# Token pairs, an earlier first group and re-placed weight requests in an FFN beside a long convolution

## The chip, the cores and the metric

The kernel runs on one core of one Trainium2 chip. The metric is device time in microseconds (us) of one execution. TensorE is written PE, its weight loads PEld, VectorE DVE, ScalarE ACT, GpSimd POOL, and SyncE SP; SP here only asks for DMA transfers.

## The reference

For 2048 tokens x of 576 channels the kernel computes a layer norm, a long convolution along the tokens (an S4 kernel applied through a Fourier transform) and a dense layer with SiLU, and adds all three paths.

```
xn  = layernorm(x)
K   = real(sum_n C * dB * exp(dt*A * l))          # 576 x 2048
A   = irfft(rfft(pad(xn)) * rfft(pad(K))) + xn * Dskip
B   = silu(xn @ w1) @ w2                          # w1 576 x 4608, w2 4608 x 576
out = x + A(xn) + B(xn)
```

Everything is float32. Matrix products are made of three products of rounded parts: each operand is split into a high part (a cast on ACT) and a low part (a subtraction on DVE).

## The kernel before

**The dense layer** (`ffn`, line 228, and `wino_ffn`, line 377) is the main program. Tokens are worked in two halves of 1024, each of two blocks `b` of 512; the 4608 hidden channels in 18 chunks `c` of four tiles of 128. A *plain* block (half, c, b) has four up products (`up`, line 278; u0 to u3; 14 matmuls of 512 columns each) and four down products (`down`, line 298; d0 to d3, one for 128 tokens; 24 matmuls of 288 columns each), which DVE adds to the running sum `acc` (line 316). A loop (line 347) writes the downs of one block and the ups of the next in the order u0, d0 to d3, u1, u2, u3. Behind each up stands a *gate*: SiLU into `gf` (line 294), a cast into `gh` (line 295), a subtraction into `gl` (line 296). `gh` and `gl` live in the pool `gp`, with six buffers of each, and a block's four are read until its d3 ends.

**The weights** are asked for by `load_w1` (line 235; one raw buffer `w1r` that holds two tiles) and `load_w2` (line 260; two raw buffers `w2r`), and split by casts (lines 255, 273) and subtractions. There are five buffers each for `w1h`, `w1l`, `w2h`, `w2l`.

**The Strassen phase.** From chunk 2 of the second half on, `wino_ffn` does both blocks together, in 14 groups n = 4 to 17 of two hidden tiles each, with seven block products in place of eight. `wino_x` (line 546) first forms the token sums S1 to S4 on DVE and ACT; its temporaries (pool `sx`) take the memory of the convolution-kernel generator, so it starts behind that generator's last store to `d1k`. For each group the raw `w1r` is cast as it is (parts "c2", "c1"), then summed in place by four DVE instructions (`sums`, lines 403 to 406), then cast again ("t13", "t24"). For the first group these steps stand ahead of the loop (lines 459 to 463), behind the gates of the last plain block, since each cast is issued behind the gate last written (line 389). Within the loop, group n holds the downs of what came before, the two splits of its own w2 tiles (both behind d0), the requests for the next two w2 tiles (both behind d1), the steps of the next group's w1, and at its end (line 536) the request for the w1 after that.

**The convolution** is the side program (`side`, line 973), woven into the main one at fixed places (line 1029). First come layer norm and transposition (`phase0`, with the raw tokens of the second half in `xj`, one buffer), then the convolution kernel (`kgen`), then 32 frequency steps (`spectral`, line 850: loads `ur` and `kr`, products pk and pu, DVE products, a product pb, a store to `d2`; `ka`, `kb`, `yh`, `yl` have one buffer each, and its pool `kl` takes the memory of `sx`), then `tail` (line 897). Only when all 32 have been stored can `conv_load` (line 944) fetch `ys`, 128 tokens at a time, six in flight; `add_conv` (line 951) multiplies them by the last Fourier matrix on parts of the PE array and adds them. Tokens 0 to 7 (times 128; `j` below) are added by `tail` to a sum read back as `r0`, tokens 8 to 15 by `down` itself, ahead of each of its last-step products (line 302).

**What sets the order.** A planner simulates the engines when the program is built and fixes one order for each engine's queue. An instruction is taken as it becomes ready there, in the order of the text; what stands under `high_priority` goes first, and what stands under `behind(ins)` follows `ins` on its engine. An instruction whose tile has no free buffer is held back by the planner. On the chip each queue then runs strictly in its order, so one that waits holds up all behind it.

Of the kernel before, what the change touches and what calls it, by code (L numbers as in the profile page):

```python
# [10 lines left out]
F32 = mybir.dt.float32  # L11
F32R = mybir.dt.float32r
# [5 lines left out]
P = 128  # L18
L = 2048
D = 576  # L20
# [21 lines left out]
def kernel(  # L42
# [185 lines left out]
    def ffn():  # L228
# [69 lines left out]
        def down(blk, jj, terms=None):  # L298
            half, c, b = blk
            j = 8 * half + 4 * b + jj  # L300
            js = slice(jj * P, (jj + 1) * P)
            if half == 1 and c == NCH - 1:
                add_conv(j, acc[j])
                conv_load(j + AHEAD)
            terms = terms or [(G[blk, t], W2[half, c, t]) for t in range(FT)]
            for h in range(2):
                hs = slice(h * HD, (h + 1) * HD)
                po = ps2.tile([P, 512], F32, tag="ps2", name="po")
                n = 0
                for gs, ws in terms:  # L310
                    for g, w in ((0, 0), (0, 1), (1, 0)):
                        pins["pe"] = nc.tensor.matmul(po[:, :HD], gs[g][:, js], ws[w][:, hs],  # L312
                                                      start=n == 0, stop=n == 3 * len(terms) - 1).ins
                        n += 1
                with tc.high_priority():
                    nc.vector.tensor_add(acc[j][:, hs], po[:, :HD], acc[j][:, hs])  # L316
# [25 lines left out]
        for t in range(FT):  # L342
            up(blocks[0], t, 256, 512)
            yield 3.0

        plain = blocks[:2 * (NCH + WINO_C)]
# [28 lines left out]
        yield from wino_ffn(load_w1, load_w2, split_w2, R1, W2, plain[-1], down)  # L375

    def wino_ffn(load_w1, load_w2, split_w2, R1, W2, before, down):
# [5 lines left out]
        G, WT = {}, {}  # L383

        def split(src, name, n):
            h = wp.tile([P, 5, P], F32R, tag="w1h", name="w1h", bufs=FT + 1)
            l = wp.tile([P, 5, P], F32R, tag="w1l", name="w1l", bufs=FT + 1)
            k = src.shape[1]
            with behind(pins["gh"]):
                nc.scalar.copy(h[:, :k], src)  # L390
            nc.vector.tensor_sub(l[:, :k], src, h[:, :k])
            WT[name, n] = h, l

        def raw(n):
            return R1[1, n // 2, n % 2 * 2]

        def sums(n):

            if n >= end:
                return  # L400
            r1 = raw(n)
            b11, b21, b12, b22 = (r1[:, k:k + 2, f:f + P] for f in (0, P) for k in (0, 2))
            nc.vector.tensor_sub(b22, b22, b12)
            nc.vector.tensor_sub(b12, b12, b11)
            nc.vector.tensor_add(b11, b22, b11)
            nc.vector.tensor_sub(b21, b21, b11)

        def prep(n, part):
            if n >= NFT // 2:
                return  # L410
            r1 = raw(n)
            if part == "c1":
                split(r1[:, 0:5, 0:P], "c1", n)
            elif part == "c2":
                split(r1[:, 2:5, P:2 * P], "c2", n)
            elif part == "t13":
                split(r1[:, 0:4, P:2 * P], "t13", n)
            elif part == "t24":
                split(r1[:, 0:4, 0:P], "t24", n)

        def unit(name, n, a):
            h, l = WT[name, n]
# [25 lines left out]
        first, end = WINO_C * FT // 2, NFT // 2  # L448

        def load(n):  # L450
            if n < end:
                load_w1(1, n // 2, n % 2 * 2)

        def second(n, i, part):
            if n < end:
# [28 lines left out]
        for n in range(first, end):  # L484
# [22 lines left out]
            yield 0  # L507
            prod(pb, unit("t13", n, 2), S3)
# [1 line left out]
                nc.vector.tensor_add(f5, pb, f5)  # L510
            d[2]()
            prep(n + 1, "c1")
            sums(n + 1)
            yield 0
            d[3]()
            yield 0

            def lower():
# [378 lines left out]
    def tail():  # L897
# [5 lines left out]
            nc.sync.dma_start(r0s[j], dr0[j * P:(j + 2) * P, :].rearrange("(i p) d -> p i d", p=P))  # L903

        def last(j):
            add_conv(j, r0s[j - j % 2][:, j % 2, :])
            conv_load(j + AHEAD)
            if j % 2:
                store(r0s[j - 1], j - 1, (nc.gpsimd,))
# [34 lines left out]
    def conv_load(j):  # L944
        if j < NJ:
            yss[j] = yp.tile([P, 4, HD], F32, tag="ys", name="ys", bufs=AHEAD)
            for h in range(2):
                nc.sync.dma_start(yss[j][64 * h:64 * h + 64],
                                  d2[j * 256:(j + 1) * 256, h * HD:(h + 1) * HD].rearrange("(q r) d -> r q d", q=4))

    def add_conv(j, dst):

        ys = yss.pop(j)
        py = [pss.tile([P, 512], F32, tag="pss", name="py") for _ in range(2)]
        first = pins["pe"]
        for n in range(8):
            q1, q2, h = n // 4, n // 2 % 2, 1 - n % 2
            o = 64 * q1 + 32 * q2
            rows = slice(64 * h, 64 * h + 64)
            with tc.high_priority() if n else nullcontext(), behind(first):  # L960
                mm = nc.tensor.matmul(py[h][o:o + 32, :HD], s4[rows], ys[rows, 2 * q2 + q1],
                                      start=True, stop=True, tile_position=(64 * h, o), skip_group_check=True)
            if n == 0:
                first = mm.ins
        for h in range(2):
            hs = slice(h * HD, (h + 1) * HD)
            nc.vector.tensor_add(dst[:, hs], py[h][:, :HD], dst[:, hs])

    def gate_of(i):

# [141 lines left out]
```

## Time and profile before

| | |
|---|---|
| device time, three runs | 1154.96 us median (1151.34 to 1156.66) |
| the profiled execution | 1158.77 us, 3.8 us above that median; span of its instructions 1157.0 us |
| plain blocks end, Strassen phase begins on PE | at about 670 us |
| last frequency step stored | at about 1084 us |
| last matmul | ends at about 1152 us |

Times in the views count from the first instruction. A row of the timeline gives start, duration, engine, source line, operation, output<-input, and in brackets the engine's idle time before it with what ended it. A row of the stage view gives, for a stretch, the busy time of each engine with its instructions, then the granted PE clock (1.00 is full), the DMA share and GB/s. A row of the waits gives total us, times, and the longest.

### The profile page before, as it was taken

What the parts mean: (1) busy time and instruction counts of PE and PEld (TensorE: products, weight loads), DVE (VectorE), ACT (ScalarE), POOL (GpSimd) and SP (SyncE); (2) the same over time, 40 slices, a digit from 0 to 9 for tenths busy, and PEclk for the clock granted to TensorE, in tenths of its full rate; (3) what the DMA queues carried; (4) which work ended last, traced back from release to release, by engine and by line L of the source; (5) the groups of instructions that cost most, each with busy time, mean ns of one, the idle gap of its engine ahead of it and who ended that gap; (6) DMA issues with size and microseconds to landing.
All of it is one profiled execution on the core that took longest, in us unless ns stands there. A gap on an engine that the chain in (4) does not pass through costs nothing.

```text
span 1157.0 us, 23107 instructions
## 1 busy us (share of the span) xinstructions
PE 1112.0 (96%) x9101; PEld 992.5 (86%) x9101; DVE 980.7 (85%) x1675; ACT 735.5 (64%) x1297; POOL 100.4 (9%) x178
## 2 busy tenths in 40 slices
PE   6999999999999999999999989999999999999988
PEld 5988898999988888888889878998898899898765
DVE  6699779999999999989999488978888789788425
ACT  4665356667776676766667347877878678677310
POOL 1110000000000000000000010111111111110102
PEclk9999999999999999999999999999999999999979
DMA  9345421424242415264743325444444445443598
GB/s 271 109 138 177 158 76 59 120 72 101 94 107 90 109 60 134 80 191 146 217 132 86 79 59 170 128 133 144 137 128 127 138 131 156 122 145 97 145 233 226
DMA packets 167372, 151.26 MB, mean 131 GB/s; under 512 B 87984, under 2 KB 136128, under 8 KB 166624
## 3 DMA queue, kind: packets, MB, share of 16 engines
q1 hardware_dynamic: 150128, 112.66, 35.0%
q0 software_dynamic: 16752, 36.24, 10.0%
q8 instruction: 72, 1.18, 0.4%
q10 hardware_dynamic: 384, 0.89, 0.3%
q14 instruction: 36, 0.29, 0.1%
HBM read 103.74 MB, written 46.08 MB: 129 GB/s over the span
## 4 chain that ended last, share of the span: by engine, by line
PE 51%; DVE 23%; DMA 10%; ACT 9%; issue 5%; SPq 1%; ACTq 0%; DVEq 0%; POOL 0%; POOLq 0%
PE po L312 22%; PE ph L286 13%; DMA w1r<-in_B_w_dram 4%; PE pb L430 3%; DVE acc L316 2%; DVE C L784 2%; DMA w2r<-in_B_w_dram 2%; DVE th L759 2%; PE kp L816 2%; PE pc L430 1%; DVE gl L296 1%; DVE S L795 1%; DVE th L776 1%; DVE C L795 1%; DMA ys<-d 1%
## 5 line engine op out<-in xcount | busy, mean ns | idle before, releaser
L312 PE MATMUL po<-w2h,gh 128*128 128x288 f32 x1152 | 342.2, 299 | 7.5 <-DVE acc L316 5.6
L312 PE MATMUL po<-w2l,gh 128*128 128x288 f32 x1152 | 339.6, 297 | 0.9 <-DVE w2l L275 0.9
L312 PE MATMUL po<-w2h,gl 128*128 128x288 f32 x1152 | 336.8, 297 | 0.6 <-DVE gl L296 0.6
L312 PEld LDWEIGHTS po<-w2h,gh 128*128 128x128 f32 x1152 | 216.9, 189 | 23.0 <-DVE acc L316 10.1
L312 PEld LDWEIGHTS po<-w2l,gh 128*128 128x128 f32 x1152 | 217.4, 189 | 7.1 <-DVE w2l L275 1.3
L312 PEld LDWEIGHTS po<-w2h,gl 128*128 128x128 f32 x1152 | 216.3, 189 | 3.7 <-issue 1.2
L316 DVE TENSOR_TENSOR acc<-po,acc 128x288 f32<-128x288 f32 x296 | 130.1, 450 | 30.9 <-PE po L312 29.5
L286 PE MATMUL ph<-xh,w1h 128*128 128x512 f32 (+1 forms) x368 | 99.3, 387 | 0.6 <-ACT xh L123 0.6
L286 PE MATMUL ph<-xl,w1h 128*128 128x512 f32 (+1 forms) x368 | 99.8, 386 | 0.0
L286 PE MATMUL ph<-xh,w1l 128*128 128x512 f32 (+1 forms) x368 | 99.8, 382 | 0.0
L294 ACT ACTIVATE gf<-ph 128x512 f32<-128x512 f32 (+1 forms) x92 | 53.2, 578 | 58.8 <-PE ph L288 53.4
L273 ACT CAST w2h<-w2r 128x576 fp32r<-128x576 f32 x72 | 47.3, 673 | 49.4 <-DMA ys<-d 26.5
L286 PEld LDWEIGHTS ph<-xl,w1h 128*128 128x128 f32 x368 | 67.3, 191 | 12.3
L286 PEld LDWEIGHTS ph<-xh,w1l 128*128 128x128 f32 x368 | 66.5, 189 | 11.7
L286 PEld LDWEIGHTS ph<-xh,w1h 128*128 128x128 f32 x368 | 65.8, 191 | 11.2 <-ACT xh L123 0.9
L777 ACT ACTIVATE c<-th 128x1040 f32<-128x1040 f32 x36 | 38.7, 1074 | 49.3 <-DVE th L776 49.2
L296 DVE TENSOR_TENSOR gl<-gf,gh 128x512 fp32r<-128x512 f32 (+1 forms) x92 | 60.5, 660 | 10.8 <-ACT gh L295 10.5
L775 ACT ACTIVATE c<-th,magic 128x1040 f32<-128x1040 f32 x36 | 42.1, 1168 | 41.5 <-DVE C L796 32.6
L853 POOL DMA_DIRECT2D m<-in_cm_dram x64 | 34.6, 542 | 308.0 <-PE pu L941 223.5
L275 DVE TENSOR_TENSOR w2l<-w2r,w2h 128x576 fp32r<-128x576 f32 x72 | 53.4, 749 | 6.2 <-ACT w2h L273 6.1
L295 ACT CAST gh<-gf 128x512 fp32r<-128x512 f32 (+1 forms) x92 | 55.1, 601 | 4.3 <-PE po L312 2.7
L157 POOL DMA_DIRECT2D d1u<-u x32 | 17.4, 543 | 453.5 <-ACT u L156 453.5
(268 smaller groups left out, 2460.3 us busy)
## 6 DMA issues: line engine op xcount, KB each, us to landing
w2r<-in_B_w_dram SPq DMA_DIRECT2D x72, 288.0 KB, 3.6
w1r<-in_B_w_dram SPq DMA_DIRECT2D x35, 512.0 KB, 3.7
d1u<-u POOLq DMA_DIRECT2D x32, 288.0 KB, 2.7
d1k<-stage SPq DMA_DIRECT2D x18, 512.0 KB, 6.9
ur<-d1u SPq DMA_DIRECT2D x32, 288.0 KB, 3.0
kr<-d1k SPq DMA_DIRECT2D x32, 288.0 KB, 2.8
d<-yo POOLq DMA_DIRECT2D x32, 288.0 KB, 2.8
ys<-d SPq DMA_DIRECT2D x32, 288.0 KB, 9.0
```

Source lines behind the costliest of these rows:

```text
L273: pins["w2h"] = nc.scalar.copy(h2, r2).ins
L275: nc.vector.tensor_sub(l2, r2, h2)
L286: nc.tensor.matmul(ph, w[:, kt, :], v[:, kt, a:e], start=n + kt == 0, stop=False)
L294: nc.scalar.activation(gf, ph, AF.Silu)
L295: pins["gh"] = nc.scalar.copy(gh, gf).ins
L296: pins["gl"] = nc.vector.tensor_sub(gl, gf, gh).ins
L312: pins["pe"] = nc.tensor.matmul(po[:, :HD], gs[g][:, js], ws[w][:, hs], start=n == 0, stop=n == 3 * len(terms) - 1).ins
L316: nc.vector.tensor_add(acc[j][:, hs], po[:, :HD], acc[j][:, hs])
L430: pins["pe"] = nc.tensor.matmul(dst, a[:, kt], v[:, kt], start=start and n == 0, stop=stop and n == 5, skip_group_check=True).ins
L775: nc.scalar.activation(c65, th, AF.Identity, bias=magic)
L777: nc.scalar.activation(c65, th, AF.Abs)
L853: nc.gpsimd.dma_start(m, cm23[:, k, i:i + 2])
```

## The change

1. `gp` has five buffers instead of six. In the Strassen phase every sixth gate takes its pair from the pool `xp` instead, which lives from there on. `xj` has two buffers instead of one.
2. The first Strassen group's request for w1 stands behind u0 of the last plain loop pass instead of u2, and its five steps stand behind d1, d2, d3, u1 and u2 of that pass instead of ahead of the Strassen loop. The request for the second group's w1 follows them, at the same place in the text.
3. In a group of the Strassen loop the second w2 split moves from d0 to d3, and each request for a w2 tile of the next group stands right behind the split of this group that frees a raw buffer.
4. In the last step, tokens 8 to 15 get their convolution two at a time, behind the product of the even one: 16 matmuls in one run, the second set in the PSUM pool `ps1`, and the two `ys` requests behind them. Tokens 0 to 7 stay as they were.

```diff
-    gp = ctx.enter_context(tc.tile_pool(name="gp", bufs=6))
+    gp = ctx.enter_context(tc.tile_pool(name="gp", bufs=5))
...
-        t = pool.tile([P, 2, D], F32, tag=tag, name=f"{tag}{j}", **({"bufs": 1} if tag == "xj" else {}))
+        t = pool.tile([P, 2, D], F32, tag=tag, name=f"{tag}{j}")
...
-            if half == 1 and c == NCH - 1:
-                add_conv(j, acc[j])
-                conv_load(j + AHEAD)
...
+            if half == 1 and c == NCH - 1 and jj % 2 == 0:
+                add_conv((j, acc[j]), (j + 1, acc[j + 1]))
+                for i in range(2):
+                    conv_load(j + i + AHEAD)
...
+        early = {"d1": "c2", "d2": "c1", "d3": "sums", "u1": "t13", "u2": "t24"}
...
-                if new == (1, WINO_C) and (b, step) == (0, "u2"):
-                    load_w1(1, WINO_C, 0)
+                if new == (1, WINO_C):
+                    if step == "u0":
+                        load_w1(1, WINO_C, 0)
+                    elif step in early:
+                        prep(first, early[step])
...
-            gh, gl = (gp.tile([P, 512], F32R, tag=n, name=n) for n in ("gh", "gl"))
+            spare = len(G) % 6 == 5
+            gh, gl = ((wino["pool"] if spare else gp).tile([P, 512], F32R, tag=n, name=n) for n in ("gh", "gl"))
...
-        for part in ("c2", "c1"):
-            prep(first, part)
-        sums(first)
-        for part in ("t13", "t24"):
-            prep(first, part)
         load(first + 1)
...
             d[0]()
             second(n, 0, "split")
-            second(n, 1, "split")
+            second(n + 1, 0, "load")
...
             d[1]()
-            second(n + 1, 0, "load")
-            second(n + 1, 1, "load")
             prep(n + 1, "c2")
...
             d[3]()
+            second(n, 1, "split")
+            second(n + 1, 1, "load")
...
-    def add_conv(j, dst):
+    def add_conv(*parts):
...
-        py = [pss.tile([P, 512], F32, tag="pss", name="py") for _ in range(2)]
+        ys = [yss.pop(j) for j, _ in parts]
+        py = [[pool.tile([P, 512], F32, tag=tag, name="py") for _ in range(2)]
+              for pool, tag in ((pss, "pss"), (ps1, "ps1"))[:len(parts)]]
...
-        for n in range(8):
-            q1, q2, h = n // 4, n // 2 % 2, 1 - n % 2
+        for n in range(8 * len(parts)):
+            i, q1, q2, h = n // 8, n // 4 % 2, n // 2 % 2, 1 - n % 2
```

More of the change, by code (lines that the diff above doesn't have):

```diff
@@ L344, in ffn, with split, raw, sums @@
             yield 3.0
+        WT = {}
+        first, end = WINO_C * FT // 2, NFT // 2
+        def split(src, name, n):
+            h = wp.tile([P, 5, P], F32R, tag="w1h", name="w1h", bufs=FT + 1)
+            l = wp.tile([P, 5, P], F32R, tag="w1l", name="w1l", bufs=FT + 1)
+            k = src.shape[1]
+            with behind(pins["gh"]):
+                nc.scalar.copy(h[:, :k], src)
+            nc.vector.tensor_sub(l[:, :k], src, h[:, :k])
+            WT[name, n] = h, l
+        def raw(n):
+            return R1[1, n // 2, n % 2 * 2]
+        def sums(n):
+            r1 = raw(n)
+            b11, b21, b12, b22 = (r1[:, k:k + 2, f:f + P] for f in (0, P) for k in (0, 2))
+            nc.vector.tensor_sub(b22, b22, b12)
+            nc.vector.tensor_sub(b12, b12, b11)
+            nc.vector.tensor_add(b11, b22, b11)
+            nc.vector.tensor_sub(b21, b21, b11)
+        def prep(n, part):
+            if n >= end:
+                return
+            if part == "sums":
+                return sums(n)
+            r1 = raw(n)
+            if part == "c1":
+                split(r1[:, 0:5, 0:P], "c1", n)
+            elif part == "c2":
+                split(r1[:, 2:5, P:2 * P], "c2", n)
+            elif part == "t13":
+                split(r1[:, 0:4, P:2 * P], "t13", n)
+            elif part == "t24":
+                split(r1[:, 0:4, 0:P], "t24", n)
+        early = {"d1": "c2", "d2": "c1", "d3": "sums", "u1": "t13", "u2": "t24"}
         plain = blocks[:2 * (NCH + WINO_C)]
@@ L372, in ffn, with wino_ffn @@
                     f(*new, t)
-                if new == (1, WINO_C) and (b, step) == (0, "u2"):
-                    load_w1(1, WINO_C, 0)
-        yield from wino_ffn(load_w1, load_w2, split_w2, R1, W2, plain[-1], down)
-    def wino_ffn(load_w1, load_w2, split_w2, R1, W2, before, down):
+                if new == (1, WINO_C):
[3 more added lines that the diff above has]
+                        prep(first, early[step])
+        yield from wino_ffn(load_w1, load_w2, split_w2, prep, WT, first, end, W2, plain[-1], down)
+    def wino_ffn(load_w1, load_w2, split_w2, prep, WT, first, end, W2, before, down):
         ps_a = ps1.tile([P, 512], F32, tag="ps1", name="pa")
@@ L382, in wino_ffn @@
         nc.tensor.matmul(ps_a, x40[:, :P], x40, start=True, stop=True)
[L383 to L419, printed above, removed]
+        G = {}
         def unit(name, n, a):
@@ L446, in gate @@
                 pins["gl"] = nc.vector.tensor_sub(gl, gf, gh).ins
-        first, end = WINO_C * FT // 2, NFT // 2
         def load(n):
@@ L454, in second @@
         def second(n, i, part):
-            if n < end:
+            if first <= n < end:
                 f = 2 * n + i
                 (load_w2 if part == "load" else split_w2)(1, f // FT, f % FT)
-        for part in ("c2", "c1"):
-            prep(first, part)
-        sums(first)
-        for part in ("t13", "t24"):
-            prep(first, part)
         load(first + 1)
@@ L512, in wino_ffn @@
             prep(n + 1, "c1")
-            sums(n + 1)
+            prep(n + 1, "sums")
             yield 0
             d[3]()
+            second(n, 1, "split")
+            second(n + 1, 1, "load")
             yield 0
@@ L905, in last @@
         def last(j):
-            add_conv(j, r0s[j - j % 2][:, j % 2, :])
+            add_conv((j, r0s[j - j % 2][:, j % 2, :]))
             conv_load(j + AHEAD)
@@ L960, in add_conv @@
             with tc.high_priority() if n else nullcontext(), behind(first):
-                mm = nc.tensor.matmul(py[h][o:o + 32, :HD], s4[rows], ys[rows, 2 * q2 + q1],
+                mm = nc.tensor.matmul(py[i][h][o:o + 32, :HD], s4[rows], ys[i][rows, 2 * q2 + q1],
                                       start=True, stop=True, tile_position=(64 * h, o), skip_group_check=True)
@@ L964, in add_conv @@
                 first = mm.ins
-        for h in range(2):
-            hs = slice(h * HD, (h + 1) * HD)
-            nc.vector.tensor_add(dst[:, hs], py[h][:, :HD], dst[:, hs])
+        for i, (_, dst) in enumerate(parts):
+            for h in range(2):
+                hs = slice(h * HD, (h + 1) * HD)
+                nc.vector.tensor_add(dst[:, hs], py[i][h][:, :HD], dst[:, hs])
     def gate_of(i):
```

1 line of the change is left out of this document (removed).

## The prediction

> **What bounds the kernel now.** I read the page first.
>
> ```profile
> span 1157.0 us, 23107 instructions
> ...
> PE 1112.0 (96%) x9101; PEld 992.5 (86%) x9101; DVE 980.7 (85%) x1675; ACT 735.5 (64%) x1297; POOL 100.4 (9%) x178
> ```
>
> PE is idle for 45 us in all, and the change removes no matmul; it can win only PE's idle time, time at a low PE clock, and overhead of small matmuls. So I cut the span into stages by what the program does in them.
>
> ```profile
> 0.00:60.00 60.00, 48.60 (x321) 44.79 (x322) 41.32 (x103) 34.24 (x65) 10.86 (x15) 1.00 0.64 183
> 60.00:200.00 140.00, 137.60 (x953) 124.66 (x952) 120.57 (x208) 76.70 (x115) 4.61 (x6) 0.99 0.40 126
> 200.00:655.00 455.00, 447.03 (x4759) 400.87 (x4758) 434.46 (x638) 310.63 (x468) 21.20 (x39) 1.00 0.41 113
> 655.00:712.00 57.00, 50.31 (x295) 43.54 (x295) 42.88 (x68) 28.36 (x50) 3.61 (x6) 0.97 0.37 92
> 712.00:1080.00 368.00, 362.81 (x2249) 330.72 (x2249) 310.96 (x595) 278.61 (x591) 48.87 (x90) 1.00 0.45 133
> 1080.00:1157.00 77.00, 65.64 (x532) 47.89 (x530) 30.50 (x66) 6.98 (x14) 11.24 (x23) 0.88 0.84 220
> ```
>
> PE's idle time is span minus its first number. The two long stages lose 8.0 us in 455 and 5.2 in 368: PE-bound. The passage from plain blocks to Strassen groups loses 6.7 in 57, the end 11.4 in 77, and these two also have a clock under 1.00. There the change works, so I asked who PE waited for: first in the passage, then at the end.
>
> ```profile
> PE pb L430 <- ACT w1h L390: 2.2, 1, 2.2
> PE po L312 <- DVE acc L316: 1.5, 2, 0.9
> PE pa L430 <- ACT pa L490: 1.5, 1, 1.5
> PE pb L436 <- DVE f L510: 1.2, 1, 1.2
> PE pu L941 <- ACT kb L871: 0.3, 1, 0.3
> ```
>
> ```profile
> PE py L961 <- DMA ys<-d: 6.6, 4, 2.6
> ```
>
> The low clock is placed by stretches.
>
> ```profile
> 698.97:702.38 3.41, 1.84 (x9) 1.09 (x8) 3.28 (x8) 3.27 (x8) 0.54 (x1) 1.00 0.03 7
> 702.38:705.80 3.42, 3.42 (x11) 2.77 (x10) 2.85 (x6) 2.77 (x5) 0.00 (x0) 0.50 0.63 196
> ...
> 1098.33:1101.74 3.41, 3.41 (x22) 2.62 (x18) 0.82 (x2) 0.00 (x0) 0.84 (x2) 0.50 1.09 219
> 1108.57:1122.22 13.65, 11.04 (x45) 7.56 (x44) 3.32 (x7) 4.03 (x8) 1.93 (x4) 0.50 0.96 240
> ```
>
> Each half-clock stretch follows one in which PE was often idle: the first follows 3.41 us with 1.84 busy. At half speed it costs 3.42 / 2 = 1.7 us; the two at the end cost up to (3.41 + 13.65) / 2 = 8.5, beside the 6.6 of waits.
>
> **Part 2, the early casts.** ACT's rows show the passage.
>
> ```profile
> 654.74 0.62 ACT L295 CAST gh<-gf 128x512 fp32r<-128x512 f32 x1
> ...
> 670.88 1.13 ACT L390 CAST w1h<-w1r 128x384 fp32r<-128x384 f32 x2
> ...
> 697.97 0.51 ACT L390 CAST w1h<-w1r 128x384 fp32r<-128x384 f32 x1 [3.14 <-DMA w1r<-in_B_w_dram]
> ```
>
> The first group's casts run at 670.88, behind the last plain gate, and PE waits 2.2 for them. In the new place they run behind gates of the block before, in an ACT that is busy 28.36 of 57 us in this stage, and less before d3. That wait goes: **2.2 us**. DVE's groups from 666.8 to 691.1 show the rest.
>
> ```profile
> L552 DVE TENSOR_TENSOR x<-xh,xl 128x1024 f32<-128x1024 f32 x4 | 4.6, 1219 | 1.7 <-DMA d1k<-stage 1.7
> L391 DVE TENSOR_TENSOR w1l<-w1r,w1h 128x512 fp32r<-128x512 f32 (+2 forms) x4 | 2.7, 685 | 0.9 <-ACT w1h L390 0.9
> ...
> L406 DVE TENSOR_TENSOR w1r<-w1r 128x256 f32<-128x256 f32 x1 | 0.4, 415 | 0.0
> L405 DVE TENSOR_TENSOR w1r<-w1r 128x256 f32<-128x256 f32 x1 | 0.4, 414 | 0.0
> L403 DVE TENSOR_TENSOR w1r<-w1r 128x256 f32<-128x256 f32 x1 | 0.4, 409 | 0.0
> L404 DVE TENSOR_TENSOR w1r<-w1r 128x256 f32<-128x256 f32 x1 | 0.4, 409 | 0.0
> ```
>
> DVE is the engine in demand here: the token sums start when the store to `d1k` has landed and then run without a pause. Four w1 subtractions (2.7) and four sums (1.6) stand among them: 4.3 us of DVE leave this stretch. They go to one where DVE waits for PE:
>
> ```profile
> 664.72 0.46 DVE L316 TENSOR_TENSOR acc<-po,acc 128x288 f32<-128x288 f32 x1 [1.15 <-PE po L312]
> ```
>
> so there they cost nothing; if that cover were gone, they cost the same 4.3. Of the 3.0 us that PE waits for `acc` and `pa`, I take half, **1.5** (bounds 0 and 3.0), since DVE keeps its long sums.
>
> The raw `w1r` is freed by the last subtraction of the first group, and SP asks for the second group's weights behind it:
>
> ```profile
> 688.80 0.33 SPq L933 DMA_DIRECT2D ur<-d1u  x1
> ...
> 691.03 0.38 SPq L242 DMA_DIRECT2D w1r<-in_B_w_dram  x1
> ```
>
> It is in time nowhere: ACT stands 3.14 us at the cast of 697.97 with the spectral copies queued behind it, DVE stands behind ACT, the addition of line 510 is late, PE waits 1.2 + 0.3 and loses 1.7 to the clock. With the group free at about 668 the request comes some 20 us sooner. This chain goes: **3.2 us** (bounds 1.5, if the clock dips anyway, and 3.2). PE's total in the passage is 2.2 + 1.5 + 3.2 = 6.9.
>
> The Trainium skill ("TensorE: Matmul & The Clock Gate", Part 1: The HAM clock gate) says that PE falls to half clock after an idle window of about 3.4 us. Here the dip came with 1.84 of 3.41 us busy, so the trace does not agree; by the rule the dip has another cause and stays, and the sum below would be 1.7 us less.
>
> Does PE's gain reach the end? The end hangs on the spectral steps: the last is stored, `ys` is fetched, PE waits.
>
> ```profile
> 1081.65 2.39 DMA d<-yo
> ...
> 1099.57 13.23 DMA ys<-d
> ```
>
> The 32 steps from 688.80 to 1081.65 take 12.3 us each and begin when the token sums give up their memory. If they begin no sooner, PE only waits longer at `ys`. They begin 4.3 us sooner by the DVE work taken out, and up to 3.1 more by the ACT wait that the first of them shares: 4.3 to 7.4. I take the middle, **5.9**, which is also under PE's 6.9.
>
> **Part 4, the pairs.** The chain of waits has the convolution's runs at the end of the program, each with the time that it adds on PE:
>
> ```profile
> 1128.46 2.81 PE py L961 x48
> ...
> 1141.10 0.65 PE py L961 x16
> ...
> 1143.53 0.62 PE py L961 x8
> ...
> 1147.68 0.62 PE py L961 x8
> ```
>
> The eight products of one j (128 tokens) are 16 instructions here. Unbroken and alone they take 0.65 us; half of them take 0.62, so a j cut into two runs costs 1.24. Between the last two rows lie four such half runs: two j. In the run of 48, 16 take 2.81 x 16/48 = 0.94. By what DVE adds behind them, j = 8 and 9 end that run, two others are cut, four stand alone: 2 x 0.94 + 2 x 1.24 + 4 x 0.65 = 7.0. In pairs of unbroken runs I take 8 x 0.65 = 5.2 and gain **1.8** (bounds 0, if the planner cuts them again, and 3.0, if the second of a pair costs only 0.50; no row has a pair from two PSUM pools). The DVE additions are the same number; the later `ys` requests (two instead of one behind an even j) concern j = 14 and 15 alone, which are used last.
>
> **Part 3, w2.** No wait of PE names w2 after 655. SP's waits from 690 to 1085:
>
> ```profile
> SPq L933 <- DVE kl L928: 125.4, 26, 9.6
> ...
> SPq L264 <- DVE w2l L275: 50.8, 11, 19.1
> ```
>
> SP stands 50.8 us at w2 requests, 19.1 of it in one piece, with `ur` and `kr` behind in the queue; they themselves mostly wait for their own buffer (125.4). I take 0; the bounds are 0 and the rival of the early spectral end below.
>
> **Part 1, buffers.** The row of 654.74 is the gate of u1, 10 us ahead of the last down's addition at 664.72: it used a sixth `gh`. With five it must wait until that block's d3 has been read. Plain blocks thus lose a cover. PE waited for `gh` and `acc` there:
>
> ```profile
> PE po L312 <- DVE acc L316: 4.1, 2, 2.4
> ...
> PE po L312 <- ACT gh L295: 0.7, 1, 0.7
> ```
>
> I take one more wait like the second, **0.7** lost (bounds 0 and the slower rival). The second `xj` lets the token loads of 60 to 200 come earlier; the longest `acc` wait of 2.4 lies in that stretch. I take 0 (bounds 0 and 2.4 gained): the DVE that is late there waits for other stores too.
>
> **Sum.** 5.9 + 1.8 - 0.7 = 7.0 us. The profiled execution took 1158.8 (span 1157.0 and 1.8 around it), which becomes 1151.8. It stood 3.8 above the median of the runs, so I forecast 1155.0 - 7.0 = **1148**; its own range is 1143 to 1153, from the bounds of the passage and of the pairs.
>
> **Rivals.** *The gain dies at the end.* If the spectral steps begin or run no sooner, only the pairs count: 1155 - 1.8, about 1153. For it: 6.6 us of `ys` waits already. Against it: the DVE rows above. This is also the time if the casts are planned late again behind the gates of u1 and u2.
>
> *The spectral steps end far sooner.* If SP's w2 waits do hold up `ur` and `kr`, (50.8 - 19.1) = 31.7 us come off the steps, `ys` lands before PE asks, and the 6.6 + 8.5 of the end go: as much as 15 more, 1133. Against it: the buffer waits of 125.4. Half of it gives 1148 - 7.5, about 1140.
>
> *Slower: five `gh` buffers.* In the stage from 200 to 655 DVE is busy 434.46 of 455 us, and it makes the convolution kernel whose last store starts the token sums. If the cast of a held gate (0.62) stands in ACT's queue ahead of that work, or late ahead of the next block's downs, each of the 21 passes can cost one wait like PE's 0.7 for `gh` above: 14.7 in place of the 0.7 taken, the whole passage slides, and the time is 1155 - 7.7 + 14.7 = 1162. It decides against the change from 7.7 / 21 = 0.37 us a pass on. For it: DVE has 20 us of slack there in all, and the planner used a sixth buffer at 654.74. Against it: what comes behind u1's gate on PE's side is two more ups, so the gate has time.
>
> **Chances.** Forecast 0.42, gain lost at the end 0.20, early spectral end 0.16, slower 0.22. Half a per cent, 5.8 us, is about what a measurement of this kernel tells from no change: faster is under 1149.2, slower over 1160.7. Faster: 0.26 of the forecast, 0.02 of the second, all 0.16 of the third, 0.44. Slower: 0.19 of the last. Same: the other 0.37. For 8 in 10 the range is 1139 to 1162: it takes in the half-way case of the early end and the slower rival.
>
> **What would show it.** Right: line 390's (now another line's) first casts end before PE's last plain up; no PE wait for `w1h`; the second w1 request near 670; the first `ur` request by about 684; no half clock near 702; four runs of 32 at the end. Wrong: the last store to `d2` as late as 1081; PE waits for `ys` above 8 us; PE idle of the stage from 200 to 655 above 12 us with `gh` or `acc` named; a last store to `d1k` later than before, which would carry everything with it. Since every queue's order is planned anew, waits may turn up in stages that no edit touches; that is what most endangers the number.

## The result and the profile after

The changed kernel took 1143.79 us, the median of four executions (1141.84 to 1145.05). The kernel before took 1154.36 on the same chip (median of four, 1151.34 to 1156.66). The ratio is 0.9908, with a 95% interval from 0.9881 to 0.9936: 10.6 us or 0.9% less. The forecast was 1148. Of the kernels below, one execution of e3 took 2764 us and counts in no ratio.

The profiled execution of after took 1145.05 us. First its page, the span and the busy times:

```profile
span 1143.3 us, 23137 instructions
...
PE 1101.7 (96%) x9101; PEld 989.3 (87%) x9101; DVE 981.5 (86%) x1675; ACT 735.9 (64%) x1297; POOL 98.5 (9%) x178
```

The span fell by 13.7 us. That is 3.1 more than the medians did: the profiled execution of before stood 4.4 above its median here, that of after 1.3. PE's idle time fell from 45.0 to 41.6, that is by 3.4; its busy time fell by 10.3 with the same 9101 matmuls. A good part of the second can be clock. The stretches at half clock, after (a last one, behind the last matmul, is left out here and before):

```profile
698.31:701.72 3.41, 3.25 (x13) 3.25 (x14) 3.17 (x6) 3.31 (x8) 0.21 (x1) 0.50 0.18 38
...
1097.67:1104.49 6.82, 6.01 (x30) 3.93 (x31) 0.91 (x2) 0.67 (x1) 0.00 (x0) 0.50 1.08 284
```

They last 10.2 us. Before there were three in the prediction's rows (3.42, 3.41 and 13.65 us) and one more:

```profile
135.77:139.18 3.41, 3.41 (x13) 2.95 (x12) 2.86 (x10) 1.61 (x3) 1.44 (x2) 0.50 0.50 152
```

That is 23.9 us. Half of the difference, 6.8 us, is the most that this can have saved: at half speed a stretch costs at most half its length. The stages of after, cut as in the prediction (the last ends with the span):

```profile
0.00:60.00 60.00, 49.02 (x325) 45.19 (x325) 41.89 (x106) 34.44 (x65) 8.63 (x15) 1.00 0.68 193
60.00:200.00 140.00, 138.30 (x963) 124.89 (x962) 128.63 (x220) 82.60 (x123) 5.64 (x6) 1.00 0.41 126
200.00:655.00 455.00, 451.15 (x4800) 405.73 (x4800) 430.83 (x635) 306.07 (x460) 20.60 (x38) 1.00 0.41 112
655.00:712.00 57.00, 50.26 (x291) 44.04 (x289) 45.57 (x72) 33.55 (x61) 4.68 (x8) 0.97 0.46 119
712.00:1080.00 368.00, 363.24 (x2270) 331.78 (x2268) 309.10 (x590) 273.92 (x582) 48.21 (x89) 1.00 0.46 135
1080.00:1143.00 63.00, 49.77 (x464) 37.72 (x464) 25.52 (x59) 5.28 (x9) 10.70 (x22) 0.94 0.89 233
```

Three things are to be seen. The passage (655 to 712), where the prediction put most of the gain, has the idle time that it had: 57.00 - 50.26 = 6.7, and the same clock, 0.97. The plain blocks (200 to 655), where it put a loss, have 3.9 us of idle time in place of 8.0. And PE ends the plain blocks sooner: the last matmuls of an up (line 288; first and last start in the view by tile) start at 662.2 in place of 669.3.

```profile
L288 PE MATMUL ph<-x,w1l x92: 279/389/398, 17.6 to 669.3; 128*128 128x512 f32 x84, 128*128 128x256 f32 x8
```

```profile
L288 PE MATMUL ph<-x,w1l x92: 278/389/478, 17.1 to 662.2; 128*128 128x512 f32 x84, 128*128 128x256 f32 x8
```

Who PE waited for in and around the passage (639 to 712), total, times and longest:

```profile
PE po L309 <- DVE acc L313: 2.7, 1, 2.7
PE pu L943 <- ACT kb L873: 2.6, 1, 2.6
PE pb L438 <- ACT s2h L559: 1.3, 1, 1.3
PE po L309 <- ACT gh L454: 0.2, 1, 0.2
```

The waits for `w1h`, `pa` and `f` are gone, and as much has come in their place: one for `acc`, since DVE's long token sums now stand closer behind PE's last plain blocks, one for a sum of tokens (`s2h`), and one for a spectral copy (`kb`). The early casts themselves ran as written. ACT's timeline of after:

```profile
639.87 0.72 ACT L355 CAST w1h<-w1r 128x640 fp32r<-128x640 f32 x1
...
655.39 0.61 ACT L355 CAST w1h<-w1r 128x512 fp32r<-128x512 f32 x1
660.65 0.62 ACT L355 CAST w1h<-w1r 128x512 fp32r<-128x512 f32 x1
...
667.96 0.52 ACT L355 CAST w1h<-w1r 128x384 fp32r<-128x384 f32 x1 [2.87 <-DMA w1r<-in_B_w_dram]
```

and SP's timeline:

```profile
662.10 1.55 SPq L242 DMA_DIRECT2D w1r<-in_B_w_dram  x1
...
684.91 0.33 SPq L935 DMA_DIRECT2D ur<-d1u  x1
```

The second group's w1 is asked for at 662.1 instead of 691.0 (ACT still stands 2.87 us at its first cast, the row of 667.96); but the first `ur`, with which the 32 spectral steps begin, comes only 3.9 us sooner. At the other end, PE's waits from 1075 on, and the chain of waits where it lists the fetch of the convolution (`r` is the sum `r0` read back) and its runs on PE:

```profile
PE py L964 <- DMA ys<-d: 8.9, 3, 3.1
```

```profile
1070.85 0.36 SPq L950
...
1075.70 11.35 DMA r<-dr
1087.06 11.29 DMA ys<-d
...
1119.54 1.19 PE py L964 x31
...
1124.62 1.16 PE py L964 x32
...
1130.76 1.17 PE py L964 x32
...
1135.30 1.20 PE py L964 x32
```

The pairs are there: four runs of 32 (one record is missing in the first). But PE waits longer for `ys` than before, 8.9 in place of 6.6.

So three times mark the end: the first `ur` request, the last store of a spectral step, and the end of the span. The view by tile gives the stores (number; least, median and longest nanoseconds of one issue; first and last start), for before and for after:

```profile
L892 POOL DMA_DIRECT2D d<-yo x32: 542/552/552, 720.4 to 1081.6; - x32
```

```profile
L894 POOL DMA_DIRECT2D d<-yo x32: 542/549/552, 713.3 to 1067.5; - x32
```

From the last store to the end of the span it is 75.4 us before (1157.0 - 1081.6) and 75.8 after (1143.3 - 1067.5): unchanged. From the first `ur` to the last store it is 392.8 before (from 688.8) and 382.6 after (from 684.9). So of the 13.7 us, 3.9 lie ahead of the first `ur` and 10.2 in the 32 steps (0.4 go back behind them). That gave the theory for the experiments: **the end follows the last spectral store**, and what moves that store moves the time. Its rivals were the prediction's own account (the early casts bring most of it), and that PE's waits in the plain blocks and the passage count one for one.

### The profile page after: what moved, and what is told of

It is laid out like the page before. It is cut to its first block, busy times and chain, and to the rows that moved or that the text cites. A ratio compares the mean times of both kernels' runs of the same rounds, so it can differ in the third digit from the quotient of the medians.

```text
span 1143.3 us, 23137 instructions
## 1 busy us (share of the span) xinstructions
PE 1101.7 (96%) x9101; PEld 989.3 (87%) x9101; DVE 981.5 (86%) x1675; ACT 735.9 (64%) x1297; POOL 98.5 (9%) x178
## 4 chain that ended last, share of the span: by engine, by line
PE 59%; DVE 18%; DMA 9%; ACT 9%; issue 3%; SPq 1%; DVEq 0%; ACTq 0%
PE po L309 26%; PE ph L286 14%; PE pb L438 3%; DMA w1r<-in_B_w_dram 3%; PE kp L818 2%; DVE acc L313 2%; PE pc L438 2%; PE z L833 1%; PE ph L287 1%; PE ph L288 1%; PE pk L943 1%; DMA dxt<-xt 1%; PE pu L943 1%; DVE w1l L356 1%; PE pb L943 1%
## 5 line engine op out<-in xcount | busy, mean ns | idle before, releaser
L286 PE MATMUL ph<-xh,w1l 128*128 128x512 f32 (+1 forms) x368 | 97.3, 382 | 0.0
```

The lines of the kernel that those rows point to most:

```text
L286: nc.tensor.matmul(ph, w[:, kt, :], v[:, kt, a:e], start=n + kt == 0, stop=False)
```

## The experiments

This table has every kernel that was run: the ratio to the kernel before on the same chip; from its profile the first `ur` request, the last spectral store, the end of the span and the distance of the last two; and the granted PE clock, a mean over its timed executions. The kernels ran on several chips, each against before on its own chip. Before took 1154.4 us on the chip of the result and 1157.4 to 1159.0 on the others, so the spans and stores of two rows can differ by some 4 us for that alone; there is one profile of each kernel. The times expected below were written for 1154 to 1155 us of before, so it is the ratio that decides.

| kernel | ratio, 95% | first `ur` | last store | span | span - store | clock |
|---|---|---|---|---|---|---|
| before | 1 | 688.8 | 1081.6 | 1157.0 | 75.4 | 0.991 |
| after | 0.9908 (0.9881 to 0.9936) | 684.9 | 1067.5 | 1143.3 | 75.8 | 0.994 |
| e1, part 1 alone | 0.9929 (0.9908 to 0.9950) | 687.0 | 1071.5 | 1148.2 | 76.7 | 0.994 |
| e2, five `gh` alone | 0.9896 (0.9872 to 0.9919) | 688.5 | 1073.7 | 1149.4 | 75.7 | 0.993 |
| e3, part 2 alone | 0.9982 (0.9962 to 1.0003) | 686.2 | 1078.1 | 1152.9 | 74.8 | 0.985 |
| e4, part 4 alone | 0.9987 (0.9972 to 1.0002) | 687.1 | 1081.0 | 1153.4 | 72.4 | 0.992 |
| e5, side work moved (a) | 1.0012 (0.9997 to 1.0028) | 691.8 | 1082.1 | 1157.0 | 74.9 | 0.984 |
| e6, side work moved (b) | 0.9990 (0.9975 to 1.0005) | 687.3 | 1079.6 | 1155.8 | 76.2 | 0.986 |
| e7, after, one `xj` | 0.9914 (0.9892 to 0.9937) | 682.1 | 1071.7 | 1144.1 | 72.4 | 0.992 |
| e8, after without part 2 | 0.9907 (0.9885 to 0.9929) | 687.2 | 1073.1 | 1146.3 | 73.2 | 0.994 |
| e9, after, two `ka` | 0.9844 (0.9811 to 0.9876) | 687.1 | 1038.3 | 1140.1 | 101.8 | 0.991 |
| e10, before, c1 and c2 swapped | 0.9946 (0.9927 to 0.9966) | 688.5 | 1077.4 | 1154.8 | 77.4 | 0.987 |
| e11, e2, c1 and c2 swapped | 0.9899 (0.9869 to 0.9929) | 685.8 | 1074.3 | 1148.0 | 73.7 | 0.992 |
| e12, before, two `ka` | 0.9932 (0.9906 to 0.9958) | 686.4 | 1046.4 | 1149.2 | 102.8 | 0.992 |

**Part 3** needed no run. The programs as built show what it does: with it alone put into before, and with it alone taken out of after, every queue is what it was.

```
before + part 3   against before: order of PE, DVE, ACT, POOL, SP the same, waits too
after  - part 3   against after:  order of PE, DVE, ACT, POOL, SP the same, waits too
```

The planner takes an instruction when it becomes ready; where the w2 requests stand in the text had no say. The re-placed weight requests of the title changed nothing on the chip.

**e1: part 1 alone** (five `gh`, a sixth pair in the Strassen phase from `xp`, two `xj`).

```diff
-    gp = ctx.enter_context(tc.tile_pool(name="gp", bufs=6))
+    gp = ctx.enter_context(tc.tile_pool(name="gp", bufs=5))
...
-        t = pool.tile([P, 2, D], F32, tag=tag, name=f"{tag}{j}", **({"bufs": 1} if tag == "xj" else {}))
+        t = pool.tile([P, 2, D], F32, tag=tag, name=f"{tag}{j}")
...
-            gh, gl = (gp.tile([P, 512], F32R, tag=n, name=n) for n in ("gh", "gl"))
+            spare = len(G) % 6 == 5
+            gh, gl = ((wino["pool"] if spare else gp).tile([P, 512], F32R, tag=n, name=n) for n in ("gh", "gl"))
```

> Before with part 1 alone (five gh/gl buffers, the spare pair from xp, two xj buffers). Theory A (the forecast: the gain comes from the early casts, 5.9 us, and the pairs, 1.8; the buffers cost 0.7): 1154 to 1156. Theory B (the buffers gave most of it, by a new order of the plain blocks): PE's idle time from 200 to 655 falls from 8.0 to about 4 us, no half clock near 136, 1145 to 1149.

It took 0.7% off, 1149.28 against 1158.29 us. The part that was to lose 0.7 us gains some 8. PE's idle time from 200 to 655 is 3.7 us and no stretch near 136 is at half clock, as theory B said.

**e2: five `gh` and the pair from `xp`, one `xj`.** The first and the third hunk of e1's diff, without the second.

> Before with five gh/gl buffers alone, xj single. Theory A: 1155. Theory B1 (the second xj is what helps): the idle time and the half clock near 132 to 139 stay, time 1153 to 1156. Theory B2 (the new order with five buffers helps): 1147 to 1150, PE idle from 200 to 655 near 4 us. The slower rival of the forecast: 1160 or more.

```profile
L893 POOL DMA_DIRECT2D d<-yo x32: 539/549/552, 721.2 to 1073.7; - x32
```

```profile
PE po L312 <- ACT gh L295: 1.8, 1, 1.8
```

It gains 1.0%, at least as much as e1, so the gain does not need the second `xj`: theory B2, and more than its time. PE's idle time from 200 to 655 is 5.0. The stores end 7.9 us sooner though they begin 0.8 us later (721.2 against 720.4). The wait feared in the prediction's slower rival came once in the plain blocks (the second fence, from 200 to 655) and not 21 times.

**e3: part 2 alone.** The five steps ahead of the Strassen loop are gone as in the change.

```diff
+        early = {"d1": "c2", "d2": "c1", "d3": "sums", "u1": "t13", "u2": "t24"}
...
-                if new == (1, WINO_C) and (b, step) == (0, "u2"):
-                    load_w1(1, WINO_C, 0)
+                if new == (1, WINO_C):
+                    if step == "u0":
+                        load_w1(1, WINO_C, 0)
+                    elif step in early:
+                        prep(first, early[step])
```

> Before with part 2 alone (request and casts of the first Strassen group in the last plain pass). Theory A: 1148 to 1149, PE idle from 655 to 712 down from 6.7 to under 2, no half clock near 702. Theory B (the token sums on DVE hold the passage, so the wait only changes its name): PE idle from 655 to 712 stays 5 to 7, first ur request some 2 to 4 us earlier, 1152 to 1155.

The ratio gives 1158.3 x 0.0018 = 2.1 us, with an interval from -0.3 to 4.4. Its stages show the passage and then the end:

```profile
655.00:712.00 57.00, 52.88 (x316) 47.40 (x317) 45.12 (x73) 30.84 (x56) 3.70 (x7) 1.00 0.46 117
...
1103.21:1127.10 23.89, 10.89 (x117) 4.12 (x117) 5.62 (x14) 0.00 (x0) 5.29 (x11) 0.50 0.88 221
```

and its waits from 1075 on:

```profile
PE py L961 <- DMA ys<-d: 15.8, 5, 7.4
PE py L961 <- DVE r L967: 3.2, 1, 3.2
```

Here the passage gains something: 4.1 us of idle time (57.00 - 52.88) in place of 6.7, and no half clock. That lies between the two theories (under 2, and 5 to 7); the time is theory B's. The first `ur` comes 2.6 us sooner and the last store 3.5. What PE is ahead beyond that it gives back at the end, standing 15.8 us at `ys` and 23.89 us at half clock with less than half of it busy.

**e4: part 4 alone.** Hunks as in the change, `add_conv` and its call in `down`.

```diff
-            if half == 1 and c == NCH - 1:
-                add_conv(j, acc[j])
-                conv_load(j + AHEAD)
...
+            if half == 1 and c == NCH - 1 and jj % 2 == 0:
+                add_conv((j, acc[j]), (j + 1, acc[j + 1]))
+                for i in range(2):
+                    conv_load(j + i + AHEAD)
```

> Before with part 4 alone (tokens 8 to 15 two per run in the last step). Both theories: the order is that of before up to the last 25 us; four runs of 32 products instructions at 1.2 us each, 1.8 us less (bounds 0 and 3.0): 1151.5 to 1154. More than 3.0 would mean that something else at the end, the additions on DVE, was shortened too.

1158.3 x 0.0013 = 1.5 us, with an interval from -0.2 to 3.2: of the forecast size, though not told from nothing. The store is where it was, and span - store is 3.0 shorter. The runs are not the unbroken 1.2 us that was expected. In the last two of the four, PE stands at `ys` behind the first six matmuls (0.63 and 0.19 us), and the chain that ends last goes through a `ys` that was asked for at 1135.8 and took 9.0 us. So the later `ys` requests, which the prediction took to be free, bound the end here.

**e5 and e6: before, planned anew.** To see what a new order does by itself, the places where side work is woven into the main program were shifted by a hair; the work is the same.

```diff
-        marks = (0.1357, 0.613, 0.855)
+        marks = (0.1385, 0.613, 0.855)
```

```diff
-        marks = (0.1357, 0.613, 0.855)
+        marks = (0.1357, 0.616, 0.855)
```

> Before with one planning number changed and nothing else: the place at which the convolution kernel's generator is woven in, 0.1357 to 0.1385 of the main program. Same work, same buffers, another order from about 330 us on. Theory P (what part 1 won is a luckier order): the last store of a spectral step moves by several us against before (1081.6), either way, and the end with it, about 75 us behind it. Theory M (five buffers and the spare pair work by a mechanism of their own in the Strassen phase): this kernel keeps the pace of before, 392 us (within 2) from the first ur request to the last store, and the time of before within 0.3%.

> Before with another planning number changed: the place where the generator's last step is woven, 0.613 to 0.616. Theory P: again another pace of the spectral steps than 392 us and another time. Theory M: 392 us within 2 and the time of before within 0.3%.

Neither moves the time by more than 0.15%. Their last stores are within 2 us of before's, and from the first `ur` to the last store they take 390.3 and 392.3: theory M.

**e7: after with one `xj`; e8: after without part 2** (the diffs of e1's second hunk and of e3, undone).

> After without the second xj buffer, all else as after. If the second xj helps, by the 2.4 us wait and the half clock near 136: 1147 to 1149. If it gives nothing beside five gh/gl buffers, as parts alone say (ratios 0.9896 without it, 0.9929 with it): 1140 to 1144.

> After without part 2, all else as after. Theory A (early casts are worth 5.9 us): 1149 to 1150. Theory B (the end follows the last store of the spectral steps, and the early casts move the first ur request by 2 to 3 us only): 2 to 4 us over after, 1145 to 1148, the last store some 2 to 4 us later than after's 1067.5.

0.9914 and 0.9907 beside 0.9908: neither part brings anything that can be measured in company with the others (each interval is about 3 us wide to either side). For e8 both theories missed: A asked for 5 to 6 us over after, B for 2 to 4.

**e9: two `ka` and `kb` in after.** If the end follows the stores, then the loop of a spectral step has to be cut. A step's first copies need `ka` and `kb`, of which there is one each, read until the last part of `yl` is made. One buffer each of `kh` and `kl` is given up for the memory.

```diff
-            ka = kl.tile([P, D], F32, tag="ka", name="ka")
-            kb = kl.tile([P, D], F32, tag="kb", name="kb")
+            ka = kl.tile([P, D], F32, tag="ka", name="ka", bufs=2)
+            kb = kl.tile([P, D], F32, tag="kb", name="kb", bufs=2)
...
-        return split_of(t, tag)
+        return split_of(t, tag, 2 if tag == "u" else 1)
```

> After with two buffers of ka and kb, and one of kh and kl in their place (the memory is the same): the next spectral step's copies no longer wait for this one's yl. Theory B (the end follows the last store of the spectral steps, which are a chain through ka on ACT and DVE of 11.6 us a step): the step falls under 11 us, the last store comes 20 us or more before after's 1067.5, PE waits for ys less than 3 us, time 1130 to 1138. Theory C (the end is bound by the fetch of ys and PE's work, and the last store only goes along): time within 0.3% of after, 1141 to 1147, though the store comes sooner.

```profile
L894 POOL DMA_DIRECT2D d<-yo x32: 539/549/552, 714.6 to 1038.3; - x32
```

```profile
PE py L964 <- DMA ys<-d: 5.3, 3, 2.8
```

This is the fastest kernel of the study, 1141.82 against 1159.01 us. The last store comes 29.2 us before after's, so the loop was what set the pace. But by the ratios (0.9844 and 0.9908) the time is only 0.64% or 7.4 us shorter than after's, and span - store grew to 101.8: the end does not follow the store that far. 0.9844 of the result's 1154.36 is 1136 us, in the range of theory B, though with more waiting for `ys` than its 3 us. PE waits only 5.3 for `ys` now, and from 1080 to its last matmul at 1135 it is busy for 54.5 of 55 us: what bounds the end now is PE's own work.

**e10 and e11: six against five buffers, planned anew in the Strassen loop.** Two steps of the next group's w1 change places, in before (e10) and in e2 (e11).

```diff
-            prep(n + 1, "c2")
+            prep(n + 1, "c1")
...
-            prep(n + 1, "c1")
+            prep(n + 1, "c2")
```

> Before with the two casts c1 and c2 of the next Strassen group changed places: same work, six gh/gl buffers, another order of the Strassen phase alone. From the first copies of ka to the last yl: 374 to 380 us as in every kernel with six, if five buffers work by a mechanism; 366 to 380, anywhere, if it is the luck of an order.

> The same two casts changed places in the kernel with five gh/gl buffers alone (e2). From the first copies of ka to the last yl: 366 to 368 us as in e2, if five buffers work by a mechanism; anywhere from 366 to 380 if it is the luck of an order. The end comes 72 to 77 us behind the last store in both of these kernels by theory B.

With six buffers this order alone takes 0.54% off; with five it changes nothing (0.9899 beside 0.9896). So half of what five buffers brought can be had by an order. The stretch that was to decide, from the first copy of `ka` to the end of the last `yl`, is 374.2 us in e10, which fits both answers. It is 369.5 in e11, outside the 366 to 368 of the mechanism. And e7, with five buffers, has 373.9. So this mark does not show a mechanism; before has 377.1, e2 366.3 and after 367.3.

**e12: two `ka` and `kb` in before**, the diff of e9.

> Before with two buffers of ka and kb and one of kh and kl, and nothing of the change (six gh/gl buffers, late casts, single tokens at the end). Theory B (after won by an earlier last store of the spectral steps): here the store also comes by 1050, and most of the gain is had without the change: ratio to before 0.986 to 0.991, 2 to 7 us behind e9's 0.9844 for the pairs and the earlier casts. Theory D (five buffers win on PE, in the plain blocks, whatever the spectral steps do): ratio 0.993 to 1.000, since PE's own work is then what is late.

```profile
L892 POOL DMA_DIRECT2D d<-yo x32: 539/549/554, 718.0 to 1046.4; - x32
```

The store comes 35.2 us sooner and the time falls by only 0.7%: theory B's time is missed, and theory D's range just takes it in. The change on top of it (e9) brings another 0.9% (0.9932 to 0.9844), as much as without. Here too PE is busy to the end, for 63.3 of 64.6 us from 1080 on, and its waits for `ys` are about the same (6.0, and 5.3 in e9), so the change's ten microseconds are PE's in this pair, and not the store's. Part of them lies ahead of the spectral steps: the last up starts at 666.9 in e12 and at 664.2 in e9, and PE's idle time from 200 to 655 is 6.9 and 3.8.

## Why the number was right and its reason was not

**Part 2, forecast 5.9: mis-sized.** Alone it brought 2.1 (-0.3 to 4.4), and in company nothing that shows (e8). The local statements held: the casts ran early, the wait for `w1h` went, the second w1 request came at 662 ("some 20 us sooner"; it was 29). The step that failed is "They begin 4.3 us sooner by the DVE work taken out, and up to 3.1 more by the ACT wait". The first `ur` moved 2.6 us in e3 and 3.9 in after; in e8, without part 2, it moved 1.6. Its request comes when DVE has made `s4l`, the last step of the token sums (687.52 + 1.21 and 688.80 before). So what counts is DVE's stretch from the first sum to the end of `s4l`, for before and for after:

```profile
666.84 4.63 DVE L552 TENSOR_TENSOR x<-xh,xl 128x1024 f32<-128x1024 f32 x4 [1.67 <-DMA d1k<-stage]
...
687.52 1.21 DVE L558 TENSOR_TENSOR s4l<-x,s4h 128x1024 fp32r<-128x1024 f32 x1
```

```profile
665.10 4.63 DVE L554 TENSOR_TENSOR x<-xh,xl 128x1024 f32<-128x1024 f32 x4 [0.45 <-DMA d1k<-stage]
...
670.92 0.55 DVE L356 TENSOR_TENSOR w1l<-w1r,w1h 128x384 fp32r<-128x384 f32 x1
...
673.86 0.41 DVE L366 TENSOR_TENSOR w1r<-w1r 128x256 f32<-128x256 f32 x1
...
676.83 0.41 DVE L367 TENSOR_TENSOR w1r<-w1r 128x256 f32<-128x256 f32 x1
...
683.63 1.21 DVE L560 TENSOR_TENSOR s4l<-x,s4h 128x1024 fp32r<-128x1024 f32 x1
```

It shrank from 21.9 to 19.7 us, by 2.2 and not by 4.3 (in e3 by 1.1). One sum and one subtraction of the first group, 1.1 us, had stood behind `s4l` before, and with its early request the second group's w1 now puts 1.4 us of its own into the stretch. The rest of the 3.9 is an earlier first sum (665.10 against 666.84), which e8 has without part 2. And what PE gained beyond went into `ys`. This is the first rival, *the gain dies at the end*, priced at 1.8 for the pairs alone; e3 shows its mechanism.

**The passage's 6.9 us of PE.** The waits named did go, but after's idle time stayed at 6.7. In e3, with six `gh`, it fell to 4.1 and the dip went. In after PE ends the plain blocks 7.1 us sooner, while DVE's sums wait for the generator's last store, issued at 657.8 and at 658.4 before; so it waits for `acc` and `kb` there. Here a wait that was taken away gave only what the next engine in line allowed.

**The dip near 702.** The prediction had it as a follower of the late w1 (1.7 us). The late w1 went and the dip came, at 698.31, behind a gap of 2.60 us at the wait for `kb`. The Trainium skill ("TensorE: Matmul & The Clock Gate", Part 1: The HAM clock gate) says that half clock follows an idle window of about 3.4 us; the traces do not agree, with a dip behind a single gap of 2.60 us (of the 3.41 us ahead of it PE was busy for 1.27). By that rule the dip was to stay, which it did, but behind another wait than before.

**Part 4, forecast 1.8: right in size.** Alone 1.5 (-0.2 to 3.2). The four runs of after add 1.19, 1.16, 1.17 and 1.20, 4.7 in all, where 5.2 was taken for the four pairs. In after span - store is not shorter; the longer `ys` waits (8.9 against 6.6) take up 2.3. That the later requests for `ys` cost nothing did not hold in e4.

**Part 3, forecast 0: right,** for a plainer reason than the one given. The queues did not change at all.

**Part 1, forecast 0.7 lost: wrong in sign, and the largest term.** Alone it gained 0.7% (e1) to 1.0% (e2), 8 to 12 us. What the row of 654.74 showed, a gate of the next block ahead of the last down's addition, is a use of the sixth buffer, and the prediction priced its loss by the one wait that it could see. The held gates are there, as a group of the page shows, before and after:

```profile
L295 ACT CAST gh<-gf 128x512 fp32r<-128x512 f32 (+1 forms) x92 | 55.1, 601 | 4.3 <-PE po L312 2.7
```

```profile
L295 ACT CAST gh<-gf 128x512 fp32r<-128x512 f32 (+1 forms) x92 | 55.3, 602 | 7.7 <-PE po L309 6.4
```

ACT now stands 6.4 us in place of 2.7 behind downs at these casts, but ACT has 36% of the span free, and PE waited for `gh` nowhere in the plain blocks of after and once, 1.8 us, in e2. So the *slower* rival, 1162, falls: its price of 0.7 a pass was not paid.

**Where part 1's gain comes from is settled only in part.** With one `ka` it goes along with the last store: the end stands 72 to 77 us behind it in all twelve such kernels, and the five-buffer kernels among them have it at 1067.5 to 1074.3, those with six at 1077.4 to 1082.1. There a PE that is ahead of the stores stands at `ys` and falls to half clock, as e3's rows show. The mean clock does not part the two kinds: it is 0.984 to 0.992 with six and 0.991 to 0.994 with five. With two `ka`, where PE's own work bounds the end, the change is worth as much (e12, e9), so the store is not the whole of it. In the plain blocks PE's idle time is 4.8 to 8.1 us in the seven kernels with six buffers and 2.2 to 5.0 in the seven with five. Yet with one `ka` that lead alone is not enough: e6, with six, starts its last up at 663.8 and gains nothing. Not shown is why five buffers bring the store sooner. That a gate which must wait leaves ACT and DVE to the spectral step's copies would be a reason; that the planner's order is only a luckier one, as in e10, would be another. The two ranges of the last store lie only 3.1 us apart (1074.3 and 1077.4), less than before's time differs from chip to chip, and the least gain with five (e1, 0.9929) overlaps in its interval that of e10 (0.9927 to 0.9966). A second `xj`, or the pair from `xp`, beside six buffers doesn't fit the memory, so six and five buffers were not compared with all else equal.

**The sum.** The forecast put 5.9 on the early casts and -0.7 on the buffers. The runs put about 2 or less on the first and 8 to 12 on the second. With the pairs the parts alone come to 12 us and more, so they do not add up to the 10.6 either. That two errors of opposite sign left 10.6 beside 7.0, and the time within the range, is luck.

**What was to be seen.** Of the signs named, the early casts, the absent `w1h` wait, the w1 request and the four runs of 32 held. The first `ur` "by about 684" came at 684.9. "No half clock near 702" and no `ys` wait above 8 failed (8.9). The last store came at 1067.5, which only the rival *the spectral steps end far sooner* had foreseen, and not by its reason: SP's waits for w2 from 690 to 1085 hardly shrank,

```profile
SPq L935 <- DVE kl L930: 106.3, 25, 7.6
...
SPq L264 <- DVE w2l L275: 49.4, 9, 19.4
```

from 50.8 to 49.4, while the steps got faster. What shrank is the wait for their own buffer, from 125.4 to 106.3. So it is not the w2 waits that the steps were freed of.

## What to carry to other kernels

Find the loop-carried chain that ends last (here the spectral steps' single `ka` and `kb`) before pricing PE's waits: a wait that goes upstream of it can come back at its end, as 15.8 us at `ys` did in e3. And test it by cutting the chain: here its end could be moved by 29 us for a gain of 7. Where a planner fixes the order, an edit is worth what it does to the queues: compare these first (part 3 changed none), and run a neutral new order as a control before a gain of half a per cent is put down to a mechanism (e10). A buffer count is not priced by the waits that name it: here ACT stood 3.7 us longer at the gates and the kernel got faster.

## What had not been expected of the hardware

The half clock comes in pieces of 3.41 us and its multiples (6.82 in after, 13.65 before, 23.89 in e3). Its starts in one trace lie whole multiples apart: in after 698.31 and 1097.67, which is 117 times 3.413; before 135.77 and 702.38, which is 166 times 3.413. So it seems to be decided window by window, and what counts is PE's work in the window and not the length of a gap. Two windows of after, one ahead of a piece at full clock and one ahead of the dip at 698.31:

```profile
667.59:671.00 3.41, 1.64 (x8) 1.01 (x6) 3.41 (x5) 1.14 (x2) 0.00 (x0) 1.00 0.09 16
694.90:698.31 3.41, 1.27 (x6) 0.86 (x6) 2.17 (x5) 3.29 (x9) 0.33 (x1) 1.00 0.57 168
```

The gap of 2.66 us at the wait for `acc` runs across the end of the first window and brings no half clock; the gap of 2.60 us at `kb` does. Cut into such windows from 106 us on, the fourteen traces have no window at full clock with under 1.5 us of matmuls that is not followed by half clock, and none over 2.6 that is; in between both occur (1.84 before the dip at 702.38).

A second set of 16 small matmuls in one run, with its outputs in another PSUM pool, costs less than the first: 16 take 0.65 us and 32 take 1.16 to 1.20, so the second adds 0.51 to 0.55.
